# Reading the key chunks of the row-mode context matmuls in the order 1, 3, 0, 2

## The chip, the cores and the metric

The kernel runs on one core of a Trainium2 chip. The metric is the time of one execution in device microseconds. Every ratio below is the mean time of one kernel's fast runs over the mean time of the other's fast runs of the same rounds, so it is not quite the ratio of the medians that stand beside it. On one core a run counts as slow only if it is over 1.5% above the fastest of its kernel.

## The reference, cut to what matters

```python
x  = A_x                                     # 2048 rows of 640
xn = layernorm(x)
q  = (xn @ wq) as 32 heads of 192
k, v = the last 512 of 2048 cached keys and values, per head
p  = softmax(q k^T / sqrt(192))              # 2048 x 512 per head
o  = p v                                     # the context: what this case is about
s  = (o, heads side by side) @ wo
g  = silu(swiglu_ffn(xn))
out = x + s * g
```

The context of a head is a sum over 512 keys. The kernel handles the keys in four chunks of 128. A sum may be taken in any order, but for rounding.

## The kernel before

The heads are handled in 16 pairs. Within a pair there are four blocks of 512 query rows (`NB` = 4, block number `i`). For each pair TensorE first runs queries and scores of all four blocks, and ScalarE turns each score chunk into exponentials, `p_t`. Then comes a *stretch*, in which the context matmuls of that pair alternate with the output projection of blocks finished earlier. Pairs 0 to 13 use a row mode: the upper and the lower 64 rows of the array work as two separate tiles, each on one half of the keys of a chunk, into two different PSUM banks. The loop over chunks is the only thing that the change touches:

```python
    def pv(i, q2):
        ...
        def part(p):
            ...
            acc = st["acc"]                       # two PSUM banks
            turn, h = divmod(p, 2)                # h: head of the pair
            for kc in range(KC):                  # four key chunks
                for n, r in enumerate((lo, hi)):  # the two row tiles
                    k = n ^ turn                  # at the turn they swap banks
                    qt = 2 * q2 + k
                    m = nc.tensor.matmul(
                        acc[:, k, h * 256 : h * 256 + Dh + 1],
                        Ps[i][kc][r, h, qt * P : (qt + 1) * P], V_p[r, kc, h, 0 : Dh + 1],
                        start=(p == 0 and kc == 0), stop=(turn == 1 and kc == KC - 1),
                        skip_group_check=True,
                    )
                    after(m, st)                  # waits for the handshake after a turn
            if p == 1:
                turned(m, st)                     # a small GpSimd memset: the handshake
            if p == 3:
                divide(i, q2, acc, ...)           # reciprocal, scaling, transpose
```

A weight load of a chunk of `p_t` comes before each matmul. The moving operand is 192 columns of values and one column of ones, whose product is the sum of the exponentials. A *couple* below means the two matmuls (one per row tile) of one chunk; there are 3584 of these matmuls, 1792 couples.

The values of a pair live in one buffer, `V_p = [128, 4 chunks, 2 heads, Dh + 2]`, and the exponentials in a pool of 16 buffers. The scores that produce them:

```python
            for kc in range(KC):
                if kc < 3 and ...: q_rows(i + 1, kc)   # queries of the next block
                scores(i, kc)                          # 6 matmuls, then the exponential on ScalarE
```

The softmax here doesn't subtract the row's maximum and nothing guards it: scores larger than these inputs give would overflow.

## Time and profile before

The median of three runs was 920.98 us (920.84 to 921.37).

| engine | busy us | share of the span of 919.1 us |
|---|---|---|
| TensorE, matmuls | 914.2 | 99% |
| TensorE, weight loads (beside matmuls) | 548.9 | 60% |
| VectorE | 601.8 | 65% |
| ScalarE | 473.9 | 52% |
| GpSimd | 85.2 | 9% |

The table says where to look, not what a change is worth. For that one reads the stage that the change touches: whether TensorE has idle time there, and if not, what sets the pace of its matmuls. The prediction does both, and shows the lines.

### The profile page before, as it was taken

The numbers are of one execution on the slowest core, as the hardware profiler recorded it, in microseconds if no ns is written. First come the engines' busy times: TensorE is split into PE (matmuls) and PEld (weight loads), VectorE is DVE, ScalarE is ACT, GpSimd is POOL, SyncE is SP. The second block draws the span as 40 slices with busy tenths as digits, with TensorE's granted clock in tenths as the row PEclk, the third lists the DMA queues.
The fourth block names the chain that finished last, engine by engine and source line by source line (L and its number), as shares of the span: only waits on it lengthen the run. The fifth ranks groups of instructions, "written<-read, shape, count | busy, mean of one in ns | idle before, by whom it ended". The sixth has DMA issues, their size and how long they took to land.

```text
span 919.1 us, 23174 instructions
## 1 busy us (share of the span) xinstructions
PE 914.2 (99%) x9920; PEld 548.9 (60%) x9920; DVE 601.8 (65%) x844; ACT 473.9 (52%) x840; POOL 85.2 (9%) x269
## 2 busy tenths in 40 slices
PE   9999999999999999999999999999999999999998
PEld 6444444465757575656565656566666666665665
DVE  6443321467677777777777777676867777777657
ACT  4222222557464646565656565655555555556471
POOL 0000000000000000000000000000000000001976
PEclk9999999999999999999999999999999999999999
DMA  9412430045352534253534343435243444443525
GB/s 299 79 35 64 92 82 0 1 75 112 54 113 50 111 51 108 54 108 54 108 58 109 57 108 52 110 53 108 56 87 73 90 77 75 91 71 102 120 59 166
DMA packets 248167, 77.53 MB, mean 84 GB/s; under 512 B 228993, under 2 KB 248065, under 8 KB 248065
## 3 DMA queue, kind: packets, MB, share of 16 engines
q1 hardware_dynamic: 245696, 73.39, 38.9%
q10 hardware_dynamic: 2368, 2.67, 0.9%
q8 instruction: 77, 1.26, 0.6%
q14 instruction: 26, 0.20, 0.1%
HBM read 38.93 MB, written 2.62 MB: 45 GB/s over the span
## 4 chain that ended last, share of the span: by engine, by line
PE 99%; DMA 1%; DVE 0%; ACTq 0%; issue 0%
PE mm L448 22%; PE sc L462 18%; PE mm L487 16%; PE sc L602 15%; PE sc L282 11%; PE mm L312 6%; PE sc L572 4%; PE sc L564 2%; PE mm L539 2%; PE mm L564 1%; DMA x_t<-in_A_x_dram 1%; PE gu L282 0%; PE mm L321 0%; PE sc L487 0%; PE sc L539 0%; PE mm L462 0%
## 5 line engine op out<-in xcount | busy, mean ns | idle before, releaser
L466 ACT ACTIVATE p_t<-sc 128x1024 bf16<-128x1024 f32 x254 | 252.9, 1022 | 120.5 <-PE sc L462 120.5
L453 DVE TENSOR_REDUCE qT<-mm 128x512 bf16<-128x1024 f32 x189 | 231.1, 1223 | 99.0 <-PE mm L448 96.5
L517 ACT ACTIVATE O_b<-mm,r 128x192 bf16<-128x192 f32 x486 | 164.6, 421 | 183.7 <-issue 136.9
L448 PE MATMUL mm<-xnT,wq_p 64*128 64x512 bf16 x1890 | 237.5, 376 | 0.0
L462 PE MATMUL sc<-qT,khat 64*128 64x512 bf16 x1524 | 198.0, 376 | 0.0
L487 PEld LDWEIGHTS <-p_t 64*128 64x128 bf16 x3584 | 159.3, 93 | 33.8
L487 PE MATMUL mm<-V_p,p_t 64*128 64x193 bf16 x3520 | 176.7, 242 | 0.0
L615 DVE TENSOR_TENSOR s_m<-s_m,sc 128x1024 f32<-128x1024 f32 x108 | 131.9, 1221 | 60.7 <-PE sc L602 52.3
L602 PE MATMUL sc<-wo_p,OT_b 64*128 64x512 bf16 x1296 | 168.8, 376 | 0.0
L448 PEld LDWEIGHTS <-wq_p 64*128 64x128 bf16 x1890 | 105.0, 94 | 98.9 <-issue 0.8
L462 PEld LDWEIGHTS <-khat 64*128 64x128 bf16 x1536 | 85.3, 94 | 80.4 <-DVE s_t L615 0.3
L602 PEld LDWEIGHTS <-OT_b 64*128 64x128 bf16 x1296 | 70.1, 94 | 44.1 <-issue 0.3
L615 DVE TENSOR_TENSOR s_t<-s_t,sc 128x512 f32<-128x512 f32 x108 | 74.2, 687 | 28.4 <-PE sc L572 26.6
L589 POOL MEMSET turn_t<- 128x1 f32 x220 | 21.6, 98 | 700.2 <-PE mm L487 506.2
L290 DVE TENSOR_TENSOR hT<-sc,sg 128x512 bf16<-128x512 f32 x46 | 31.7, 692 | 81.5 <-ACT sg L289 81.5
L289 ACT ACTIVATE sg<-sc 128x512 bf16<-128x512 f32 x46 | 27.3, 596 | 69.8 <-PE sc L282 69.8
L282 PE MATMUL sc<-xnT,wu_sb 128*128 128x512 bf16 (+1 forms) x260 | 60.5, 355 | 0.0
L282 PE MATMUL sc<-xnT,wg_sb 128*128 128x512 bf16 (+1 forms) x260 | 60.3, 355 | 0.1
L572 PE MATMUL sc<-OT_b,wo_p 64*128 64x512 bf16 (+1 forms) x345 | 50.3, 376 | 0.0
L312 PE MATMUL mm<-wd_sb,hT 128*128 128x512 bf16 x192 | 43.9, 379 | 0.0
L282 PEld LDWEIGHTS <-wu_sb 128*128 128x128 bf16 x285 | 27.2, 98 | 26.8 <-issue 0.2
L282 PEld LDWEIGHTS <-wg_sb 128*128 128x128 bf16 x285 | 27.2, 98 | 26.3
(83 smaller groups left out, 418.8 us busy)
## 6 DMA issues: line engine op xcount, KB each, us to landing
wo_p<-in_A_wo_dram SPq DMA_DIRECT2D x16, 480.0 KB, 4.8
K_p<-in_A_k_cache_dram SPq DMA_DIRECT2D x32, 192.0 KB, 4.6
V_p<-in_A_v_cache_dram SPq DMA_DIRECT2D x32, 192.0 KB, 3.6
wq_p<-in_A_wq_dram SPq DMA_DIRECT2D x64, 80.0 KB, 2.9
wq_p<-in_A_wq_dram SPq DMA_DIRECT2D x16, 160.0 KB, 3.2
x_t<-in_A_x_dram SPq DMA_DIRECT2D x13, 160.0 KB, 3.2
x_b<-in_A_x_dram SPq DMA_DIRECT2D x4, 512.0 KB, 6.4
OT_b<-O_b SPq DMA_TRANSPOSE x124, 2.8
```

What stands on the lines that cost most here:

```text
L282: nc.tensor.matmul(out, w_sb[:, c, f * P : (f + 1) * P], xnT[:, c, qc], start=(c == 0), stop=(c == NC - 1),)
L290: nc.vector.tensor_tensor(hTs[b][:, f, :], u, sg[:], ALU.mult)
L312: nc.tensor.matmul(dn, at, by, start=(f == 0), stop=(f == NF - 1))
L448: nc.tensor.matmul(q_ps[:, h, :], pairs[pr]["wq"][r, c, j * P : (j + 1) * P], xnT[r, c, b * 512 : (b + 1) * 512], start=(c == 0), stop=(c ...
L453: nc.vector.reduce_sum(qTs[i][:, j, :], q_ps[:, :, :].rearrange("p h n -> p n h"), axis=AX.X)
L462: nc.tensor.matmul(sc[:, h, :], khat[r, j, ks], qT[r, j, :], start=(j == 0), stop=(j == 2))
L466: nc.scalar.activation(p_t[:, :, :], sc[:, :, :], ACT.Exp, scale=scale)
L487: m = nc.tensor.matmul(acc[:, k, h * 256 : h * 256 + Dh + 1], Ps[i][kc][r, h, qt * P : (qt + 1) * P], V_p[r, kc, h, 0 : Dh + 1], start=(p ...
L517: nc.scalar.activation(O_b[:, qt, h, :], a_k[:, h, 0:Dh], ACT.Copy, scale=r[:, k, h, :])
L572: nc.tensor.matmul(ps.rearrange("p (t q) -> p t q", q=P), pairs[i // NB]["wo"][r, j, MC:D], OTs[i][:, :, :].rearrange("p (t j) q -> p j t ...
L602: m = nc.tensor.matmul(ps[:, k, :], OTs[i][r, 3 * (2 * half + k) + j, :], pairs[i // NB]["wo"][r, j, MAIN], start=(turn == 0 and j == 0), ...
L615: nc.vector.tensor_tensor(to, to, ps, ALU.add)
```

## The change

The intent is to read the chunks in another order, 1, 3, 0, 2. The flag that begins an accumulation moves to the chunk that now comes first, and the flag that ends it to the one that now comes last.

```diff
+    KORDER = (1, 3, 0, 2)
+
     def pv(i, q2):
 ...
-            for kc in range(KC):
+            for kc in KORDER:
 ...
-                        start=(p == 0 and kc == 0), stop=(turn == 1 and kc == KC - 1),
+                        start=(p == 0 and kc == KORDER[0]), stop=(turn == 1 and kc == KORDER[-1]),
```

## The prediction

> **What bounds the kernel now.** I first read the page's head, to see which engine fills the span, and its row of slices, to see whether that holds everywhere.
>
> ```profile
> span 919.1 us, 23174 instructions
> PE 914.2 (99%) x9920; PEld 548.9 (60%) x9920; DVE 601.8 (65%) x844; ACT 473.9 (52%) x840; POOL 85.2 (9%) x269
> ...
> PE   9999999999999999999999999999999999999998
> ...
> PEclk9999999999999999999999999999999999999999
> ...
> PE 99%; DMA 1%; DVE 0%; ACTq 0%; issue 0%
> ```
>
> TensorE has work in flight for 914.2 of 919.1 us, at full clock in every slice, and the chain that ended last (the fourth fact) is 99% TensorE. The question is where the other 4.9 us are, and whether the changed matmuls lie near them. I cut the span at the first row-mode stretch and at the last one, and added two whole periods of one pair of heads:
>
> ```profile
> core 0: us, PE busy (x) PEld busy (x) DVE busy (x) ACT busy (x) POOL busy (x), PEclk, DMA share, GB/s
> ...
> 465.86:512.80 46.94, 46.94 (x598) 29.68 (x595) 34.64 (x45) 26.76 (x49) 1.57 (x16) 1.00 0.41 81
> 512.80:559.74 46.94, 46.94 (x598) 29.71 (x595) 34.63 (x45) 26.78 (x49) 1.57 (x16) 1.00 0.40 82
> ```
>
> Each period is 46.94 us long and TensorE is busy for 46.94 us of it. A third window, from 17.00 to 841.38 us, gave 824.38 us busy in 824.38 us, so all of the idle time is in the first 17 us (first loads and normalisation) and after 841 us (last pair of heads and stores). The row-mode context matmuls run from 190.4 to 817.2 us, inside the part with no idle time at all.
>
> A busy TensorE can still be a slow one, since pipelined matmuls overlap in the record. So I counted what a period holds and asked what the matmuls cost from start to start. By the source, a pair of heads has 12 query units of 10 matmuls, 16 score units of 6, and 4 blocks of 30 output-projection matmuls: 336 with 512 columns; and 4 blocks of 64 context matmuls: 256 with 193 columns. In the chain in order of time, a run of 12 wide ones is 1.29 us (0.1079 us each) and a run of 32 narrow ones 1.33 to 1.34 us (0.0417 us each). 336 x 0.1079 + 256 x 0.0417 = 36.25 + 10.68 = 46.93 us, against the 46.94 us of the period. Nothing is left over for a wait: the period is the sum of columns streamed, two row tiles at a time.
>
> The line of the changed matmuls itself:
>
> ```profile
> engine op xcount: duration ns min/median/max, first and last start us, forms
> L487 PEld LDWEIGHTS <-p_t x3584: 92/93/94, 190.1 to 817.1; 64*128 64x128 bf16 x200
> L487 PE MATMUL mm<-V_p,p_t x3520: 241/242/244, 190.4 to 817.2; 64*128 64x193 bf16 x196
> ...
> its engine sat idle before it (us, times) until:
> who waited for it (us, times):
>   POOL turn_t L589: 507.4, 112
>   DVE r L506: 15.6, 57
> ```
>
> Three things to see: the duration of a matmul spreads over 3 ns, and that of a weight load over 2 ns, whatever the key chunk; nothing stands under "sat idle before it"; and only two kinds of instruction wait for these matmuls, the small handshake memset and the reciprocal. Both wait for the last matmul of a group, not for a chunk in the middle.
>
> **What the Trainium skill says.** "TensorE: Matmul & The Clock Gate", section "Back-to-back issue gap", gives N/2.4 + 2.5 ns at full clock: 82.9 ns for 193 columns and 215.8 ns for 512. This trace has 1.33/16 = 83.1 ns and 1.29/6 = 215 ns per couple of row tiles, so it agrees, with both tiles of a couple in the time of one. The formula knows of columns, not of the order of chunks. "PSUM — Partial Sum Buffer", "The four PSUM rules", says that the first-matmul flag clears the written marks of a whole bank, and that a matmul without it overwrites where the mark is clear and adds where it is set. So the flag has to sit on whichever chunk comes first, in the first head only. The change moves it there, and I expect a correct result. "TensorEngine Tiling (Array Packing)", "Gotcha 1: PSUM Pressure", says that different row tiles must not access one bank at a time; that is why there is a handshake at the turn, and the change leaves it where it is. "SBUF — State Buffer", "SBUF: two separate sides", says that TensorE's reads wait on no other engine or DMA; the 241 to 244 ns agree, while the DMA share of the periods was 0.40 to 0.41.
>
> **The change part by part.**
> Removed: no instruction. Added: none. I built both kernels and compared their instruction streams: 19842 rows on TensorE in each, the same row by row, with the same kinds of waits on the same rows. Only the buffer names inside the rows are permuted. Of these rows, 3584 matmuls and 3584 weight loads belong to the changed line (14 pairs of heads x 256). The last two pairs use another, full-height form and are not touched.
>
> Time of the 3584 matmuls: 14 x 10.68 us = 149.5 us before. After: the same number, the same 193 columns and alternation of row tiles, so 149.5 us. Difference 0.
>
> Time of the weight loads: each context matmul has its own before and after, 93 ns long, overlapped with the streaming. No two neighbours share a weight, in either order, so none can be dropped. Difference 0.
>
> Waits at the head of a group: before, chunk 0 comes first and its row carries the waits for the value load, the accumulator or the handshake. After, chunk 1 is there and carries the same ones. In the new order chunk 3, the newest of a block, is read second. The closest call is the last block of a pair. The exponential of its chunks 2 and 3 ends at 559.13 + 1.94 = 561.07 us; the context matmuls of that block are in the last quarter of a stretch that runs from 559.6 to 583.2 us, hence not before about 577 us. That is some 16 us of slack, and the streams have no wait for an exponential tied to a chunk. The values are loaded whole per head (all four chunks in one transfer): issued at 544.87 us, landing 3.6 us later by the median, first read at 559.56 us, 11 us of slack. Difference 0.
>
> Release at the tail of a group: the group still ends after the same 16 couples, so the reciprocal and the handshake start when they did. The probability buffers come free in another order inside 0.7 us, but there are 16 of them and the next writer of one comes most of a period later: the exponential waits for scores alone,
>
> ```profile
> L466 ACT ACTIVATE p_t<-sc 128x1024 bf16<-128x1024 f32 x254 | 252.9, 1022 | 120.5 <-PE sc L462 120.5
> ```
>
> all 120.5 us of its idle time being put down to the score matmuls. Difference 0.
>
> Sum: 0 us on the path that sets the end, and 0 beside it. Predicted time: 920.98 + 0 = 921.0 us.
>
> **The rivals.**
> (1) Slower by a late chunk. If the second couple of each stretch had to wait for the newest exponential, the worst would be the 561.07 - 559.56 = 1.5 us by which it ends after the stretch began, 14 times: 21 us, 942 us in all (2.3% slower). Against it: the stretch begins with block 0, whose last exponentials ended at 541.65 + 1.94 = 543.59 us, 16 us earlier, and the compared streams show no such wait.
> (2) Faster by fewer or shorter waits. If there were a wait per chunk, the second chunk would cover two of them. But the line has no idle time to give, and the period's sum closes to 0.01 us. Even all the 4.9 us of idle time in the kernel are 0.5%, and they lie outside the changed stretch. At most 916 us, and I see no way to it.
> (3) An address effect. A value row is 2 x 194 x 2 = 776 bytes per chunk, so chunks 1 and 3 start 8 bytes off the 16-byte grid of chunks 0 and 2; the new order puts like by like. If phase or repetition cost anything, the old trace's durations would fall in two groups; they spread over 3 ns. If every one of 1792 couples paid 2.5 ns more, it would be 4.5 us: 925.5 us, 0.5%.
> (4) The sums are rounded in another order. This touches the last bits of the result, not the time.
>
> **Range and chances.** The three runs of before span 920.84 to 921.37 us. With an effect of 0, what is left is the spread between executions and chips, which I take as about that much on either side: 920.4 to 921.8 us. A result 2% off would need 18.4 us; rival (1) alone could bring that, and it is contradicted by the streams. Faster by over 2% needs more than the kernel's whole idle time. I give 0.985 to within 2%, 0.01 to slower and 0.005 to faster.
>
> **What would show it.** In the changed profile: a period of 46.94 us with TensorE busy for all of it; the changed line (two lines further down) with 241/242/244 ns, no idle time before it, and the same two waiters; runs of 32 context matmuls in 1.33 us; exponentials waiting for scores alone. I am wrong if the period differs by over 0.05 us (14 times that is 0.7 us), if idle time appears before the context matmuls or their weight loads, if the matmuls' durations split in two, or if the clock row falls below full.

## The result, and the profile after

The changed kernel took 921.11 us (median of 4 runs, 920.86 to 921.28), the kernel before 921.00 us in the same rounds (4 runs, 920.84 to 921.37). The ratio is 1.000, with a 95% interval of 0.9983 to 1.0018: the same.

The head of the page of the changed kernel (busy time, share of the span and number of records per engine, then the busy tenths by slices):

```profile
span 919.1 us, 23152 instructions
PE 912.8 (99%) x9898; PEld 548.9 (60%) x9920; DVE 601.8 (65%) x844; ACT 474.4 (52%) x840; POOL 85.2 (9%) x269
...
PE   9999999999999999999999999999999999999998
```

The span is the same to the tenth. TensorE seems to have lost 1.4 us of busy time, but look at the counts: 9898 matmul records against 9920 before, while the weight loads, one for each matmul, are 9920 in both. The program did not shrink; 22 records are missing from this trace, and the idle time that shows in their place is not idle.

The same two periods of one pair of heads as before, in the changed kernel:

```profile
465.86:512.80 46.94, 46.94 (x598) 29.69 (x594) 34.64 (x46) 26.80 (x49) 1.57 (x16) 1.00 0.41 81
512.80:559.74 46.94, 46.94 (x598) 29.72 (x594) 34.63 (x46) 26.80 (x49) 1.57 (x16) 1.00 0.40 82
```

TensorE (the second number) is again busy for all of both. And the changed line itself, whose number is two higher:

```profile
L489 PEld LDWEIGHTS <-p_t x3584: 92/94/94, 190.1 to 817.0; 64*128 64x128 bf16 x200
L489 PE MATMUL mm<-V_p,p_t x3520: 241/243/244, 190.3 to 817.1; 64*128 64x193 bf16 x196
...
its engine sat idle before it (us, times) until:
who waited for it (us, times):
  POOL turn_t L591: 507.4, 112
  DVE r L508: 15.5, 57
```

Nothing stands under "sat idle before it", the same two kinds of instruction wait for the line, and for as long. From the first context matmul of one stretch to the first of the next, the records of both kernels give 46.940 us.

To see inside a group, I took from both traces the time from the start of one couple to the start of the next, averaged over the 224 groups of each head (for the last chunk of head 1: to the next matmul of any kind):

```
chunk in order of reading      ns, head 0                      ns, head 1
before: 0, 1, 2, 3             83.1   85.8   82.5   82.5       82.5   86.7   82.5   82.5
after:  1, 3, 0, 2             84.0   83.1   83.1   83.1       86.6   82.5   82.5   82.5
```

In these two orders one chunk of the four is slower than the others, chunk 1, by some 4 ns in head 1, whether it comes second or first (e1 below shows that this is no rule). I had not seen it before the result. It stands in the durations too, once they are sorted by chunk: before, in head 1, every matmul of chunk 1 is on record with 244 ns, every one of chunk 2 with 241 ns and every one of chunk 3 with 242 ns. Only the range over all chunks hides it.

### The profile page after: what moved, and what is told of

Same layout as the page of the kernel before. It is cut to its first block, busy times and chain, and to the rows that moved or that the text cites. A ratio compares the mean times of both kernels' runs of the same rounds, so it can differ in the third digit from the quotient of the medians.

```text
span 919.1 us, 23152 instructions
## 1 busy us (share of the span) xinstructions
PE 912.8 (99%) x9898; PEld 548.9 (60%) x9920; DVE 601.8 (65%) x844; ACT 474.4 (52%) x840; POOL 85.2 (9%) x269
## 4 chain that ended last, share of the span: by engine, by line
PE 99%; DMA 1%; DVE 0%; ACTq 0%; issue 0%
PE mm L448 22%; PE sc L462 18%; PE mm L489 16%; PE sc L604 15%; PE sc L282 11%; PE mm L312 6%; PE sc L574 4%; PE sc L566 2%; PE mm L541 2%; PE mm L566 1%; DMA x_t<-in_A_x_dram 1%; PE gu L282 0%; PE mm L321 0%; PE sc L489 0%; PE sc L541 0%
```

## The experiments

The theory is that in this stage the time is the sum of columns streamed through TensorE, with nothing waiting for a particular chunk, so that the order is free. Three kinds of rival stand against it: that a late chunk makes the order matter, that addresses do, or that weight loads rather than columns set the pace. e0 to e3 ran on one chip beside nine runs of the kernel before (median 921.24 us, 920.58 to 922.58), e4 to e7 on another beside seven (median 921.01 us, 920.67 to 921.48). The rounds gave five runs of each of the first four kernels and four of each of the others.

### e0: the change once more

No edit; five rounds, for a closer interval.

> The changed kernel again, in five rounds beside the kernel before. My theory (the time is the sum of columns streamed, which the order does not touch): 921.0 us, ratio 1.000 within 0.0005. Rival, an address effect or a small wait of up to 2.5 ns per couple of row tiles: up to 925.5 us, ratio 1.005.

Measured: 921.28 us (920.68 to 921.94), ratio 0.9997 (0.9985 to 1.0010). The period was 46.940 us. An effect of the size of the address rival, 0.5%, is outside the interval.

### e1: the reverse order

```diff
-    KORDER = (1, 3, 0, 2)
+    KORDER = (3, 2, 1, 0)
```

> Chunk order 3, 2, 1, 0, so that the newest chunk is read first everywhere. My theory: 921.0 us, ratio 1.000 within 0.0005, since the newest chunk is ready some 16 us before it is read. Rival of the late chunk: if the slack were not there, 1.5 us in each of 14 stretches, 942 us.

Measured: 922.00 us (921.36 to 922.17), ratio 1.0005 (0.9991 to 1.0018). The median is 0.8 us above that of before; does that come from the order? The period is 46.943 us, 3 ns more, which over 14 pairs is 0.04 us. In the profiled run the first context matmul starts at 190.745 us, against 190.355 us in the first profile of before: 0.39 us that cannot come from a line which has not run yet. The rest is within the spread of before. So the reverse order is free as well, though it reads the newest chunk first.

The slow couple has moved, though. In head 1 it is now that of chunk 3, which comes first, with 85.6 ns, while chunk 1 takes 82.6 ns. The sum hardly moves: the eight couples of both heads take 668.1 ns before, 667.5 ns in the order 1, 3, 0, 2 and 667.8 ns here.

### e2: value rows on 16-byte boundaries

```diff
-    V_p = consts.tile([P, KC, 2, Dh + 2], bf, name="V_p")
+    V_p = consts.tile([P, KC, 2, Dh + 8], bf, name="V_p")     # from the kernel before, order 0, 1, 2, 3
```

> Order 0, 1, 2, 3 as before, but each head's value row is padded from 194 to 200 elements, so that every chunk and head starts on a 16-byte boundary. My theory (addresses play no part): 921.0 us, durations still 241 to 244 ns. Rival of the address effect: some of the 1792 couples get faster by up to 2.5 ns, down to 916.5 us.

Measured: 921.07 us (920.46 to 921.32), ratio 0.9994 (0.9981 to 1.0006). The line of the context matmuls in this run:

```profile
L487 PE MATMUL mm<-V_p,p_t x3520: 243/243/244, 190.9 to 817.5; 64*128 64x193 bf16 x196
```

The durations lie within 1 ns, and the gaps between couples are 83.3 ns for every chunk. So the slow chunk is an effect of the layout, and it is gone with the padding. But the other chunks have become 0.8 ns slower at the same time, and the period is 46.927 us: 0.013 us a pair, 0.2 us a kernel. The rival is right that addresses play a part, and wrong about its size. Which couple is slow depends on the order too (e1), but the sum over a group hardly does. Being off the 16-byte grid is not enough by itself: in the old layout chunks 1 and 3 of a head start equally far off it, and in head 1 only one of them is slow in each order. Whether it is the step from row to row, the start of the buffer or that of some neighbour which also moved, this run does not separate.

### e3: 200 columns in place of 193

```diff
-    V_p = consts.tile([P, KC, 2, Dh + 2], bf, name="V_p")
+    V_p = consts.tile([P, KC, 2, Dh + 8], bf, name="V_p")
-        nc.gpsimd.memset(V_p[:, :, :, Dh : Dh + 2], 1.0)
+        nc.gpsimd.memset(V_p[:, :, :, Dh : Dh + 8], 1.0)
-                        acc[:, k, h * 256 : h * 256 + Dh + 1],
-                        Ps[i][kc][r, h, qt * P : (qt + 1) * P], V_p[r, kc, h, 0 : Dh + 1],
+                        acc[:, k, h * 256 : h * 256 + Dh + 8],
+                        Ps[i][kc][r, h, qt * P : (qt + 1) * P], V_p[r, kc, h, 0 : Dh + 8],
```

> The rows are padded as in the run before, and the 3584 context matmuls stream 200 columns in place of 193 (the seven more are ones and their results are never read; the result stays right). My theory, columns streamed: 1792 couples x 7 / 2.4 ns = 5.2 us more, 926.2 us. Rival, that weight loads of 93 ns set the pace of these matmuls and hide the streaming: no change, 921.0 us.

Measured: 925.50 us (924.78 to 926.78), ratio 1.0043 (1.0030 to 1.0056). The stage does pay for columns, and weight loads do not hide them. Against e2, which has the same layout, it is 4.4 us more. The gap between couples is 85.83 ns for every chunk, 2.5 ns above e2's 83.33, and 1792 x 2.5 ns = 4.5 us closes the sum. I had expected 7 columns / 2.4 = 2.92 ns; seven columns cost as much as the prediction's rate of 2.4 columns per ns gives for six. Why, no run here shows.

### e4: 128 columns for most of them

```diff
                     qt = 2 * q2 + k
+                    w0 = 0 if turn == 0 and kc == 0 else 65
-                        acc[:, k, h * 256 : h * 256 + Dh + 1],
-                        Ps[i][kc][r, h, qt * P : (qt + 1) * P], V_p[r, kc, h, 0 : Dh + 1],
+                        acc[:, k, h * 256 + w0 : h * 256 + Dh + 1],
+                        Ps[i][kc][r, h, qt * P : (qt + 1) * P], V_p[r, kc, h, w0 : Dh + 1],
```

> Wrong result on purpose: of the 32 matmuls into an accumulator, 28 stream 128 columns (65 to 192) in place of 193, the first four stay whole so that every column is written. My theory, columns streamed: 1568 couples x 65 / 2.4 ns = 42.5 us less, 878.5 us. Rival, that weight loads have no room left beside shorter matmuls: they stay at the pace of 83 ns a couple, 921 us, or something between if they bind partly.

Measured: 882.31 us (881.57 to 882.74), ratio 0.9582 (0.9566 to 0.9598). So 38.7 of the expected 42.5 us came. From the couple of chunk 2, one of the fast ones, to the next it is 55.84 ns in place of 82.5: weight loads of 93 ns, two in each couple, still leave room. Summed over a group and all 448 groups, the gaps between couples shrink by 41.5 us. So 1.0 us of the 3.8 us missing were lost to gaps that shrank a little less than I had reckoned. Another 1.2 us are a new wait, by which three of the periods are longer than the others (by 0.45, 0.50 and 0.23 us); the first of them and the period after it:

```profile
318.91:363.39 44.48, 44.18 (x599) 24.44 (x595) 34.08 (x45) 26.76 (x48) 1.60 (x16) 1.00 0.49 86
363.39:407.43 44.04, 44.04 (x599) 25.10 (x595) 34.08 (x45) 26.76 (x48) 1.60 (x16) 1.00 0.48 86
```

In the first of the two TensorE is busy for 44.18 of 44.48 us. What it waited for there, from the view of waits in that window:

```profile
PE sc L603 <- DMA OT_b<-O_b: 0.3, 1, 0.3
```

The output projection waits for the transposed context, which the DMA brings: with 6% off the period, this transfer begins to show. I have not traced the last 1.6 us in full. Some of it lies at the first stretch: from its first context matmul to that of the next pair the time shrank by 2.58 us, where an ordinary period shrank by 2.91 us, and the trace has a wait of TensorE for VectorE there, of 0.21 us at 199.5 us.

This run carries a warning. Its result is wrong (65 of the 192 columns of each head miss most of their sum), and the comparison with the reference passed it all the same. So that comparison does not see even gross errors in the context sums; the output is `x + s * g`, and I take it that `s * g` is small beside `x`, without having measured it.

### e5, e6, e7: the slack taken away

By the prediction, the order is free because every chunk is ready long before it is read. So I took the slack away: in pairs 1 to 13 the scores are computed in the block order 1, 2, 3, 0, and the stretch, which begins with block 0, now begins with the exponentials just issued. The instruction streams now show waits for an exponential on the weight loads of chunks, where there were none.

```diff
+    SEQ = [
+        pr * NB + b for pr in range(NPAIR)
+        for b in (range(NB) if pr == 0 or pr >= last - 1 else (1, 2, 3, 0))
+    ]
+    NEXT = dict(zip(SEQ, SEQ[1:]))
-    EARLY = (NB + 1, 1)
+    EARLY = (SEQ[NB + 1], 1)
 ...
-            i = pr * NB + b
+            i = SEQ[pr * NB + b]
             for kc in range(KC):
-                if kc < 3 and i + 1 < NS and (i + 1, kc) != EARLY:
-                    q_rows(i + 1, kc)
+                if kc < 3 and i in NEXT and (NEXT[i], kc) != EARLY:
+                    q_rows(NEXT[i], kc)
```

e5 has this edit in the kernel before (0, 1, 2, 3); e6 in the changed kernel (1, 3, 0, 2); e7 in the changed kernel with `KORDER = (3, 2, 1, 0)`.

> Takes away the slack: in pairs 1 to 13 the scores are computed in the block order 1, 2, 3, 0, so that the stretch begins with the block whose exponentials have just been issued. Chunk order 0, 1, 2, 3. By the old trace chunk 3 of that block is ready 1.51 us after the stretch begins; its first couple would be due after 3 x 0.083 us, so TensorE waits 1.26 us in each of 13 stretches, with some 0.1 us to start again: 16 to 18 us, 937 to 939 us. Rival, that a wait there is absorbed by other work: 921 us.

> As the run before, with chunk order 1, 3, 0, 2: chunk 3 is due as the second couple, 0.083 us after the beginning, so the wait is 0.17 us longer per stretch: 2.2 us above the run before, 939 to 941 us. If the order of chunks plays no part even without slack: the same as the run before.

> As the two runs before, with chunk order 3, 2, 1, 0: chunk 3 is due at once, so the wait is 0.25 us longer per stretch than with 0, 1, 2, 3: 3.2 us above that run, 940 to 942 us. If the order of chunks plays no part even without slack: the same as that run.

| run | order | median us (range) | ratio (95%) | period us | more than 46.940 | x 13 |
|---|---|---|---|---|---|---|
| e5 | 0, 1, 2, 3 | 937.97 (937.75 to 938.33) | 1.0185 (1.0170 to 1.0200) | 48.253 | 1.313 | 17.1 |
| e6 | 1, 3, 0, 2 | 940.72 (940.11 to 941.25) | 1.0214 (1.0199 to 1.0229) | 48.420 | 1.480 | 19.2 |
| e7 | 3, 2, 1, 0 | 943.16 (941.81 to 945.37) | 1.0243 (1.0228 to 1.0258) | 48.507 | 1.567 | 20.4 |

The beginning of a stretch before, from the timeline of TensorE (start, duration, what):

```profile
559.56 1.51 PE L487 MATMUL mm<-V_p,p_t 64*128 64x193 bf16 x32
```

Thirty-two context matmuls follow each other without a break. The beginning of a stretch in e5, from the timeline of all engines; what ended an idle time stands in brackets:

```profile
519.70 1.94 ACT L466 ACTIVATE p_t<-sc 128x1024 bf16<-128x1024 f32 x2 [0.70 <-PE sc L462]
...
520.14 0.33 PE L487 MATMUL mm<-V_p,p_t 64*128 64x193 bf16 x4
...
520.78 0.26 PE L487 MATMUL mm<-V_p,p_t 64*128 64x193 bf16 x2 [0.31 <-ACT p_t L466]
...
521.69 1.26 PE L487 MATMUL mm<-V_p,p_t 64*128 64x193 bf16 x26 [0.66 <-ACT p_t L466]
```

Chunks 0 and 1 run, chunk 2 waits for the first of the two exponentials, and chunk 3 and all that follows wait for the second, which ends at 519.70 + 1.94 = 521.64 us. The same place in e7:

```profile
522.66 1.94 ACT L466 ACTIVATE p_t<-sc 128x1024 bf16<-128x1024 f32 x2 [0.70 <-PE sc L462]
...
524.66 1.51 PE L489 MATMUL mm<-V_p,p_t 64*128 64x193 bf16 x32 [1.39 <-ACT p_t L466]
```

Here chunk 3 comes first, and nothing runs before 522.66 + 1.94 = 524.60 us. And in e6, with the changed order, where chunk 1 runs and chunk 3 waits:

```profile
521.12 1.94 ACT L466 ACTIVATE p_t<-sc 128x1024 bf16<-128x1024 f32 x2 [0.70 <-PE sc L462]
...
521.57 0.25 PE L489 MATMUL mm<-V_p,p_t 64*128 64x193 bf16 x2
...
523.12 1.43 PE L489 MATMUL mm<-V_p,p_t 64*128 64x193 bf16 x30 [1.30 <-ACT p_t L466]
```

In all three the stretch really goes on 0.05 to 0.06 us after the newest exponential. What the order decides is how many couples are done by then: three in e5, one in e6, none in e7. Two couples are 0.167 us, and e6's period is 0.167 us above e5's; three couples by the gaps of chunks 0, 1 and 2 are about 0.25 us, and e7's is 0.254 us above. The totals of e5 and e6 follow (17.1 and 19.2 us against 17.0 and 19.7 of the medians). Those of e7 do less well: 20.4 us by the periods against 22.2 us of the medians, and its 943.16 us lie above the 940 to 942 us expected. Its own rounds spread over 3.6 us, and its profiled run starts its first context matmul at 191.421 us, 1.07 us later than the first profile of before; that much is not in the period, and I have not looked for its cause.

The idle time in brackets, 0.31 + 0.66 us, is less than the 1.313 us that the period grew by. A matmul is on record for some 0.242 us, but with nothing to wait for the next couple starts 0.083 us after it. So at each of the two waits some 0.16 us of standing still count as busy, and 0.97 + 0.32 = 1.29 us is close to the growth. The period is the safer measure.

## Why the prediction was right

**The bound.** Right. The claim that the period is the sum of columns, with nothing left for waits, is now tested from both sides: more columns lengthened it (e3), fewer shortened it (e4), and both by the measured gap times the number of couples, but for the DMA wait that e4 uncovered and its 1.6 us that are not traced in full. One figure of the sum can't be had from the lines shown: 1.29 us for 12 wide matmuls are 0.1075 us each, not 0.1079. The trace bears it out all the same: in the two periods from 465.86 to 559.74 us it is 0.1079 us by the mean from the start of a wide matmul to the next start, and 0.0418 us from that of a narrow one.

**Nothing removed or added; weight loads, heads and tails of groups unchanged.** Right. The periods of both kernels are equal to the nanosecond and the same two kinds of instruction wait.

**16 us of slack for the newest chunk.** Right, and shown to be the condition: with the slack there the reverse order is free (e1), without it the order is worth up to 0.254 us per stretch. The changed order, applied there, costs 0.167 us a stretch more than the old one.

**The rival of the late chunk.** The prediction put its worst at 1.5 us for each of 14 stretches. When I produced that wait in 13 stretches, it was 1.480 us each in the changed order, of which the rival spoke, and 1.567 us in the worst one. So the size was right and its absence was the point.

**The rival of the address effect.** The verdict was right, a detail of the argument was not. I wrote that "the old trace's durations would fall in two groups; they spread over 3 ns", and took this as evidence against the effect. That reading failed: the prediction also says that a duration spreads "whatever the key chunk", but sorted by chunk the durations do fall in groups (244 ns for chunk 1 of head 1, 241 ns for chunk 2), and the couple of chunk 1 takes 86.7 ns there in place of 82.5. It does not matter, because the sum over a group is nearly the same in all three orders (the periods are 46.940, 46.940 and 46.943 us) and because removing the effect (e2) gave only 0.2 us. That the sums agree is measured and not explained. The prediction did not foresee it, so on this rival its zero was in part luck.

**A correct result.** The comparison with the reference passed, but e4 shows that it would have passed a broken sum as well. That the start flag sits rightly on chunk 1 therefore rests on the argument of the prediction, and no run here shows it.

**The range.** 921.11 and 921.28 us lie in 920.4 to 921.8 us. Single runs went slightly outside it, to 921.94 us, as did those of the kernel before on that chip, to 922.58 us.

## What to carry to other kernels

Before asking what an order of work is worth, ask whether anything waits for one item of it: compare the time at which the last item is ready with the time at which it is first read, and look for waits on that line. Where there is slack, a permutation of the same instructions is worth nothing; where there is none, read the newest item last, and it is worth the number of items that can run meanwhile times the time of one. An engine that is busy all through a repeating period can be checked by a sum (instructions times their start-to-start time), and a change is worth what it does to the terms of that sum, until something else has to be waited for, as in e4.

## What the Trainium skill lacked or had wrong

- "TensorE: Matmul & The Clock Gate", "Back-to-back issue gap": it gives N/2.4 + 2.5 ns for one matmul to the next, which holds here to 1 ns for most couples (82.5 or 83.3 ns at 193 columns against 82.9, 85.83 at 200 against 85.83, 55.84 at 128 against 55.83). It has no term for the layout of the moving operand, and no page gives a size for one: with rows of 388 bytes the slow couple of head 1 took 85.6 to 86.7 ns by the order and the others some 82.5 ns, with rows of 400 bytes all took 83.3 ns. It calls the formula that of an isolated matmul and says that a stream of weight load and matmul pairs sustains about 81 ns a matmul at 128 columns; in e4, couples of two half-height matmuls, with a weight load before each, started 55.84 ns apart where no slow chunk was read, as the formula has it.
- The same page, "LDWEIGHTS (loading the stationary operand)": columns over 1.2, by which I estimate 107 ns for 128 columns. The weight loads of this line, of half the rows, took 92 to 94 ns, and those of full height in the last two pairs 95 to 99 ns.
